# PSUM banks by role instead of by turn, in the groups of seven products

## The chip, the cores and the metric

The kernel runs on one core of a Trainium2 chip. The metric is the device time of one execution in microseconds (us), the median of several executions. A profile is one further execution that the hardware profiler recorded; its rows are in us from the start of the recorded span unless marked ns. Engine names are those of the profile: PE is the matrix engine's matmuls, PEld its weight loads (they run beside the matmuls), ACT the scalar engine, DVE the vector engine, POOL the GpSimd engine, SP the engine that issues most DMAs.

## The reference

One normalised input `xn = layernorm(x)` of 2048 tokens and 576 features goes through two branches, whose results are added to `x`.

```python
def _A_ref(x, wqkv, wo):      # 32 heads of 18; each token sees 8 tokens, 2 apart
    ...
    return o @ wo
def _B_ref(x, w1, w2, w3, w4):
    h = _gelu(_layernorm(x) @ w1)
    ...                       # four quarters of h shifted by +1, -1, +2, -2 tokens
    x1 = x + hs @ w2
    h2 = _gelu(_layernorm(x1) @ w3) @ w4     # 576 -> 4608 -> 576
    return x1 + h2
return x + _A_ref(xn, A_wqkv, A_wo) + _B_ref(xn, B_w1, B_w2, B_w3, B_w4)
```

The change lies in the last matmul pair, `gelu(layernorm(x1) @ w3) @ w4`, which is the largest part of the work.

## The kernel before

**Stages.** The order of the instructions on each engine is written out by hand. In time there come: the qkv projection, the mixing with `w1` and `w2`, the large MLP with the attention running on DVE beside it, and at the end the projection with `wo` (L1298 to L1325) with the output. All matmuls take their operands as a high and a low part, each in a reduced float format.

**The MLP in two forms.** The 36 blocks of 128 hidden features are taken as 18 pairs. The first 12 pairs (`NPL`) are computed directly. The last 6 pairs (`NWP`) are computed in groups, one per pair and half of the tokens: 12 groups, `q` = 0 to 11, in the loop at L1110. A group is a fast 2x2 scheme (after Strassen and Winograd) that needs seven block products in place of eight. Each product (`product`, L1051) is seven matmuls of 128x512 into one PSUM bank. Sums of weights and of inputs were made ahead (`combine`, `sums`), so a group is seven products with some additions of their results.

**Results and banks.** The seven products go to three banks:

- `ca` takes P1, then P6, P7 and P4 are added onto it, one after the other. Between them ACT copies out what stands there: `keep(Z1, ca)` after P1, `keep(Z2, ca)` after P6, `keep(Z3, ca)` after P7. Each later product onto `ca` therefore waits for the copy before it. What stands there after P4 is one quarter of the result: at the head of the next group ACT applies gelu to it twice (`gelu_ps("c21", ca, Z4)`, L1115, the instructions of L783 and L784), and that is the last use of the bank.
- `cb` takes P2 alone; DVE adds it to Z1 (`z_add(Z1, cb, Z1)`).
- `cc` takes P5, is read by DVE (`z_add(Z3, cc, Z3)`), has P3 added onto it, and is read by DVE for the last time in `z_add(Z2, cc, Z2)`.

A counter hands out four banks in turn (`cc0` to `cc3`, L1054 and L1055). With three requests per group, the bank that `cb` of a group gets is the one that `ca` of the group before had; `cc` gets the one that `cb` of the group before had, and `ca` gets the one that `cc` had two groups before. A first matmul into a bank waits until the bank's last reader is done.

**Order within a group.** Between the products stand up to eight `down` steps (L807), D0 to D7, which multiply the hidden features of the group before by `w4`: twelve matmuls of 128x288 each into one of two double banks, read out by DVE (L827) or by ACT into a staging tile (L823) that a POOL DMA adds onto `yd` in HBM (L824). The order is a string:

```python
ORDER = "P1 P2 P6 P5 P7 D0 P4 D1 P3 D2 D3 D4 D5 D6 D7"
ORDERS = {0: "P1 P2 D0 P6 P5 P7 D1 D2 P3 P4 D3",
          1: "P1 P2 D0 P6 D1 P5 P7 D2 P4 D3 P3 D4 D5 D6 D7",
          NWP - 1: "P1 P2 P6 P5 P7 D0 P4 P3 D1 D2 D3 D4 D5 D6 D7",
          NWP: "D0 D1 P1 P2 D2 P6 D3 P5 P7 D4 P4 P3 D5 D6 D7"}
```

Other work is hung on these steps by a plan (L1153 to L1237): the gelus of the finished quarters (`gelu_z`, L789 and L790, with `low_part`, L794, on DVE), the loads and the splitting of weights (`split_w4`, L562 and L564; `split_a` and `split_s`, L911 to L916), and in groups 2, 3, 5 and 6 `split_op` (L876 to L880), which splits the inputs of the second half of the tokens. ACT and DVE execute all this strictly in the order in which it is issued.

After group 11 come the last `gelu_ps` (L1267), eight last `down` steps (L1277) and the projection with `wo`.

Of the kernel before, what the change touches and what calls it, by code (L numbers as in the profile page):

```python
# [8 lines left out]
F32 = mybir.dt.float32  # L9
# [48 lines left out]
def fused_block(ctx, tc, x, wqkv, wo, w1, w2, w3, w4, out):  # L58
# [376 lines left out]
    T4 = mpool.tile([128, S + 4], F32R, name="T4")  # L435
# [180 lines left out]
    for t in range(NT):  # L616
        ps = psb.tile([128, 2, 512], F32, name="ps", tag="b")
# [169 lines left out]
    def gelu_z(name, z):  # L787
        h = hp.tile([128, 2, 512], F32R, name=name, bufs=2 if name == "c11" else 1)
        act.activation(h[:, 0, :], z, AF.Gelu_apprx_tanh)  # L789
        act.activation(z, z, AF.Gelu_apprx_tanh)  # L790
        return h

    def low_part(h, g):
        dve.tensor_tensor(h[:, 1, :], g, h[:, 0, :].bitcast(F32), op=ALU.subtract)  # L794
# [7 lines left out]
        h = hid[u, i] = gelu_ps((("c12", "c22"), ("c21", "c11"))[u % 2][i], ps, g)  # L802
        low_part(h, g)

    nps = [0, 0]

    def down(t, parts, pd):  # L807
        col = slice(t % 4 * 128, (t % 4 + 1) * 128)
        if pd is None:
            nps[0] += 1  # L810
            ps = qpd.tile([128, 2, 512], F32, name=f"ps{nps[0] % 2}")
        else:
            ps = pd.tile([128, 2, 512], F32, name="ps", tag="b")
        seq = []
        for h, w in parts:
            seq += [(h[:, 0], w, 0), (h[:, 0], w, 1), (h[:, 1], w, 0)]
        for n, (h, w, p) in enumerate(seq):
            for k in range(2):
                pe.matmul(ps[:, k, :HF], h[:, col], w[:, p, k * HF:(k + 1) * HF],  # L819
                          start=n == 0, stop=n == len(seq) - 1)  # L820
        if t in YD:
            e = staging()
            act.copy(e.rearrange("p (h c) -> p h c", h=2), ps[:, :, :HF])  # L823
            pool.dma_start(yd[t], e, accum_op=ALU.add)  # L824
        else:
            yv = Y[:, t, :].rearrange("p (h c) -> p h c", h=2)
            dve.tensor_tensor(yv, ps[:, :, :HF], yv, op=ALU.add)  # L827
# [215 lines left out]
    qpc = qpcc.__enter__()  # L1043
# [4 lines left out]
    SLOT = {"A11": 0, "A22": 1, "A12": 2, "S1": 0, "S3": 1, "S2": 2, "S4": 3}  # L1048
    WX = {}

    def product(w, xk, onto=None, last=False):  # L1051
        ps = onto
        if ps is None:
            nps[1] += 1  # L1054
            ps = qpc.tile([128, 512], F32, name=f"cc{nps[1] % 4}")  # L1055
        for i, (a, v) in enumerate(HALVES):
            k = 128 if a else 96
            pe.matmul(ps, WX[w][:k, v, SLOT[w], :], area[sb][xk][:k, a, :],  # L1058
                      start=onto is None and i == 0, stop=last and i == len(HALVES) - 1,
                      skip_group_check=True)  # L1060
        return ps

    def keep(z, ps):
        act.copy(by_token(z), in_order(ps))

    def z_add(dst, ps, z):
        dve.tensor_tensor(by_token(dst), in_order(ps), by_token(z), op=ALU.add)
# [42 lines left out]
    for q in range(NQ):  # L1110
# [126 lines left out]
            at("P5", lambda: read_xo(1, ring_block(("o", 1))))  # L1237
        for it in ORDERS.get(q, ORDER).split():
            if it == "P1":
                ca = product("A11", "B11")  # L1240
                keep(Z1, ca)
                if q:
                    low_part(h21, Z4)
            elif it == "P2":
                cb = product("A12", "B21", None, True)
                z_add(Z1, cb, Z1)
            elif it == "P6":
                product("S2", "T2", ca)
                keep(Z2, ca)
            elif it == "P5":  # L1250
                cc = product("S1", "T1")
                h11 = hid[q, "c11"] = gelu_z("c11", Z1)
            elif it == "P7":
                product("S3", "T3", ca)
                keep(Z3, ca)
                z_add(Z3, cc, Z3)
                low_part(h11, Z1)
            elif it == "P4":
                product("A22", "T4", ca, True)
            elif it == "P3":  # L1260
                product("S4", "B22", cc, True)
                z_add(Z2, cc, Z2)
            else:
                down(*prev[int(it[1])], None)
            for f in plan.get(it, ()):
                f()
# [31 lines left out]
    for t in range(NT):  # L1298
# [14 lines left out]
        if t < NT - 1:  # L1313
            ps = psb.tile([128, 2, 512], F32, name="ps", tag="b")
# [40 lines left out]
```

## Time and profile before

| | us |
|---|---|
| median of 3 runs | 1297.74 |
| lowest and highest of them | 1296.04, 1299.88 |
| the profiled execution's own time | 1297.46 |
| its recorded span | 1295.7 |
| PE busy | 1274.2 |
| DVE busy | 921.3 |
| ACT busy | 558.4 |
| POOL busy | 214.4 |

The twelve groups take the stretch from 925.67 us to 1218.34 us of the span. In a row of the timeline stand the start, the length, the engine, the line, the operation, the tiles written and read, the shape and the count of merged instructions; in brackets at the end stands the time that the engine sat idle before it and what ended that. A row of waits gives the total, the count and the longest. Matmuls are pipelined, so the lengths of consecutive ones overlap and the distance of their starts is what counts.

### The profile page before, as it was taken

The page shows a single profiled execution, that of the slowest core. Times are in us where ns is not written, and L with a number is a line of the kernel's source. Part 1 is how long each engine was busy: PE and PEld are TensorE (multiplying, and loading weights), DVE is VectorE, ACT ScalarE, POOL GpSimd, SP SyncE. Part 2 cuts the span into 40 slices and gives each one's busy share as a digit, 9 for nine tenths or more (in the row PEclk, how much of TensorE's full clock was granted, in tenths as well). Part 3 has the DMA queues.
Part 4 walks back from the last instruction along what each step waited for, and adds up shares of the span by engine and source line. Part 5 has one row for each costly group of instructions (what it writes and reads, how often), then busy time and mean ns, then how long its engine had stood idle before and what let it go on. Part 6 is the DMA issues. An engine that isn't in the chain of part 4 may idle for free. (4 is left out here: it accounts for less than half of the span.)

```text
span 1295.7 us, 19586 instructions
## 1 busy us (share of the span) xinstructions
PE 1274.2 (98%) x7594; PEld 1168.2 (90%) x7594; DVE 921.3 (71%) x1307; ACT 558.4 (43%) x900; POOL 214.4 (17%) x318
## 2 busy tenths in 40 slices
PE   8999999999999999999999999999999999999998
PEld 8999998898898999999998989988888898898998
DVE  6456534778568999999999999976855656676441
ACT  4322226526634434343434343434855466455530
POOL 2011100021221212221212221111111112112100
PEclk9999999999999999999999999999999999999999
DMA  7646874246896887986867877558747587788982
GB/s 209 155 115 142 171 169 144 72 140 173 199 261 142 179 195 156 190 172 136 187 142 157 172 142 153 97 108 194 195 78 156 111 192 144 164 202 180 260 255 82
DMA packets 196172, 210.21 MB, mean 162 GB/s; under 512 B 77920, under 2 KB 134176, under 8 KB 195952
## 3 DMA queue, kind: packets, MB, share of 16 engines
q1 hardware_dynamic: 165536, 144.82, 38.9%
q0 software_dynamic: 30544, 64.16, 32.0%
q8 instruction: 59, 0.97, 0.3%
q14 instruction: 33, 0.27, 0.1%
HBM read 112.98 MB, written 107.28 MB: 170 GB/s over the span
## 5 line engine op out<-in xcount | busy, mean ns | idle before, releaser
L819 PEld LDWEIGHTS ps<-w,c 128*128 128x128 f32 x3456 | 466.6, 188 | 15.0 <-DVE Y L827 4.7
L819 PE MATMUL ps<-w,c 128*128 128x288 f32 x3456 | 473.1, 294 | 6.1 <-DVE Y L827 3.5
L824 POOL DMA_DIRECT2D yd<-Y x125 | 109.2, 876 | 451.8 <-ACT Y L823 413.6
L823 ACT COPY Y<-ps 128x576 f32<-128x576 f32 x125 | 79.9, 640 | 162.6 <-PE ps L819 80.9
L794 DVE TENSOR_TENSOR c<-Y,c 128x512 fp32r<-128x512 f32 x144 | 98.9, 687 | 58.7 <-ACT Y L784 50.0
L783 ACT ACTIVATE c<-p 128x512 fp32r<-128x512 f32 x96 | 57.6, 600 | 190.8 <-PE p L800 190.8
L212 PE MATMUL ps<-WQ,xt 128*128 128x432 f32 x672 | 134.8, 360 | 0.0
L212 PEld LDWEIGHTS ps<-WQ,xt 128*128 128x128 f32 x672 | 125.6, 188 | 5.7
L726 DVE TENSOR_TENSOR prod<-q,k 128x1152 f32<-128x1152 f32 x64 | 86.6, 1353 | 11.1 <-DMA k<-qkvd 10.4
L827 DVE TENSOR_TENSOR Y<-ps,Y 128x576 f32<-128x576 f32 x108 | 81.1, 751 | 17.0 <-PE ps L819 16.8
L729 DVE TENSOR_REDUCE L<-prod 128x64 f32<-128x1152 f32 x64 | 86.4, 1351 | 1.1
L824 POOL DMA_DIRECT2D yd<-ev x55 | 47.8, 888 | 223.5 <-ACT ev L823 222.6
L800 PE MATMUL p<-xt,w3a 128*128 128x512 f32 x336 | 79.0, 391 | 1.4 <-ACT Y L784 1.4
L800 PE MATMUL p<-xt,w3s 128*128 128x512 f32 x336 | 78.6, 390 | 0.0
L800 PE MATMUL p<-x1n,w3a 128*128 128x512 f32 x336 | 78.5, 390 | 0.0
L800 PE MATMUL p<-x1n,w3s 128*128 128x512 f32 x336 | 78.5, 390 | 0.0
L705 DVE TENSOR_TENSOR prod<-v,L 128x1152 f32<-128x1152 f32 x56 | 75.8, 1353 | 0.8
L709 DVE TENSOR_TENSOR o<-o,prod 128x1152 f32<-128x1152 f32 x56 | 75.8, 1353 | 0.6
L800 PEld LDWEIGHTS p<-xt,w3a 128*128 128x128 f32 x336 | 62.2, 188 | 14.9 <-ACT Y L784 2.2
L119 POOL TENSOR_TENSOR rs<-rs,mhalf 128x1 f32<-128x1 f32 x48 | 31.0, 645 | 260.5 <-DVE rs L118 148.0
L800 PEld LDWEIGHTS p<-xt,w3s 128*128 128x128 f32 x336 | 62.4, 188 | 12.6
L800 PEld LDWEIGHTS p<-x1n,w3a 128*128 128x128 f32 x336 | 62.4, 188 | 12.6
(196 smaller groups left out, 1759.6 us busy)
## 6 DMA issues: line engine op xcount, KB each, us to landing
yd<-Y POOLq DMA_DIRECT2D x127, 288.0 KB, 5.4
yd<-ev POOLq DMA_DIRECT2D x55, 288.0 KB, 5.2
Y<-in_B_w_dram SPq DMA_DIRECT2D x23, 576.0 KB, 6.9
w3st<-in_B_w_dram SPq DMA_DIRECT2D x44, 256.0 KB, 6.0
qkvd<-stg SPq DMA_DIRECT2D x24, 432.0 KB, 3.5
xd<-st SPq DMA_DIRECT2D x16, 320.0 KB, 6.0
xd<-big SPq DMA_DIRECT2D x16, 320.0 KB, 7.5
xin<-in_A_x_dram SPq DMA_DIRECT2D x16, 288.0 KB, 3.9
```

Of the source, the lines that this page charges most:

```text
L212: pe.matmul(ps[:, h, :n], xs(a), ws(b, h), start=i == 0, stop=i == len(PAIRS) - 1)
L705: dve.tensor_tensor(dst, vv, Lf[:, :, w:w + 1].to_broadcast([128, TPP * GH, HD]), op=ALU.mult)
L709: dve.tensor_tensor(o, o, dst, op=ALU.add)
L726: dve.tensor_tensor(prod.rearrange("p (j h) d -> p j (h d)", h=GH), q, k[:, r0:r0 + TPP, :], op=ALU.mult)
L729: dve.tensor_reduce(Lf[:, :, w], prod, axis=AX.X, op=ALU.add)
L783: act.activation(by_token(h[:, 0, :]), in_order(ps), AF.Gelu_apprx_tanh)
L794: dve.tensor_tensor(h[:, 1, :], g, h[:, 0, :].bitcast(F32), op=ALU.subtract)
L800: pe.matmul(ps, W3[f][:, w, :], x1n[b][:, a, :], start=n == 0, stop=n == len(PAIRS) - 1)
L819: pe.matmul(ps[:, k, :HF], h[:, col], w[:, p, k * HF:(k + 1) * HF], start=n == 0, stop=n == len(seq) - 1)
L823: act.copy(e.rearrange("p (h c) -> p h c", h=2), ps[:, :, :HF])
L824: pool.dma_start(yd[t], e, accum_op=ALU.add)
L827: dve.tensor_tensor(yv, ps[:, :, :HF], yv, op=ALU.add)
```

## The change

The counter of banks goes. `product` is told the bank: `ca` takes bank 0 in even groups and bank 3 in odd groups, `cb` always takes bank 1 and `cc` always bank 2. Nothing else is altered: the order of the instructions on every engine is the same, and PE alone has other waits.

```diff
-    nps = [0, 0]
+    nps = [0]
...
-    def product(w, xk, onto=None, last=False):
+    def product(w, xk, bank=None, onto=None, last=False):
         ps = onto
         if ps is None:
-            nps[1] += 1
-            ps = qpc.tile([128, 512], F32, name=f"cc{nps[1] % 4}")
+            ps = qpc.tile([128, 512], F32, name=f"cc{bank}")
...
             if it == "P1":
-                ca = product("A11", "B11")
+                ca = product("A11", "B11", q % 2 * 3)
...
             elif it == "P2":
-                cb = product("A12", "B21", None, True)
+                cb = product("A12", "B21", 1, last=True)
...
             elif it == "P6":
-                product("S2", "T2", ca)
+                product("S2", "T2", onto=ca)
...
             elif it == "P5":
-                cc = product("S1", "T1")
+                cc = product("S1", "T1", 2)
...
             elif it == "P7":
-                product("S3", "T3", ca)
+                product("S3", "T3", onto=ca)
...
             elif it == "P4":
-                product("A22", "T4", ca, True)
+                product("A22", "T4", onto=ca, last=True)
             elif it == "P3":
-                product("S4", "B22", cc, True)
+                product("S4", "B22", onto=cc, last=True)
```

In the program before, the first matmul of P2 of groups 1 to 11 carries a wait for ACT (in group 1 for an earlier matmul too). In the changed program no matmul of P1, P2 or P5 of these groups carries a wait for the readers of its bank, since earlier waits cover them. The first matmul of D0 of group 1, which waited for DVE, waits for ACT instead. The waits of P6, P7, P4 and P3 stay as they were.

## The prediction

> **What bounds the kernel now.** I read the page's busy shares first, then the waits in the stretch of the twelve groups (915 to 1215 us), then PE's timeline there, and last what ACT did while PE waited.
>
> ```profile
> span 1295.7 us, 19586 instructions
> ...
> PE 1274.2 (98%) x7594; PEld 1168.2 (90%) x7594; DVE 921.3 (71%) x1307; ACT 558.4 (43%) x900; POOL 214.4 (17%) x318
> ```
>
> PE is busy for 1274.2 of 1295.7 us. Only PE's idle time, 21.5 us in all, can be won by moving waits.
>
> ```profile
> PEld cc L1058 <- ACT Y L784: 10.8, 10, 2.9
> ...
> PE cc L1058 <- ACT Y L784: 6.3, 8, 2.5
> ...
> PE ps L819 <- ACT ev L823: 0.4, 1, 0.4
> ...
> PE ps L819 <- DVE Y L827: 0.2, 1, 0.2
> ```
>
> In that stretch PE waits for hardly anything but one thing: the second of the two gelus that read the `ca` of the group before (L784). It is the last reader of the bank that P2 gets. Ten times the weight loads stand still for it, eight times a gap shows on PE, up to 2.5 us. These are the waits that the change takes out.
>
> A gap understates a stall, because a matmul's recorded length hides the first part. So I go by the distances of starts:
>
> ```profile
> 943.45 3.74 PE L1058 MATMUL cc<-x1n,w3a 128*128 128x512 f32 x14
> 947.03 1.75 PE L819 MATMUL ps<-w,c 128*128 128x288 f32 x12
> ...
> 967.81 1.79 PE L1058 MATMUL cc<-x1n,w3a 128*128 128x512 f32 x7
> 969.82 1.87 PE L1058 MATMUL cc<-x1n,w3a 128*128 128x512 f32 x7 [0.23 <-ACT Y L784]
> 971.53 3.39 PE L1058 MATMUL cc<-xt,w3s 128*128 128x512 f32 x14
> 974.76 1.77 PE L1058 MATMUL cc<-x1n,w3s 128*128 128x512 f32 x7
> ...
> 992.29 1.79 PE L1058 MATMUL cc<-x1n,w3a 128*128 128x512 f32 x7
> 996.53 1.86 PE L1058 MATMUL cc<-x1n,w3a 128*128 128x512 f32 x7 [2.46 <-ACT Y L784]
> 998.23 3.39 PE L1058 MATMUL cc<-xt,w3s 128*128 128x512 f32 x14
> ...
> 1045.69 1.79 PE L1058 MATMUL cc<-x1n,w3a 128*128 128x512 f32 x7
> 1047.70 1.87 PE L1058 MATMUL cc<-x1n,w3a 128*128 128x512 f32 x7 [0.23 <-ACT Y L784]
> ```
> ```profile
> 1095.21 3.79 PE L1058 MATMUL cc<-x1n,w3a 128*128 128x512 f32 x14
> 1098.84 3.45 PE L1058 MATMUL cc<-xt,w3s 128*128 128x512 f32 x14
> 1102.13 1.80 PE L1058 MATMUL cc<-x1n,w3s 128*128 128x512 f32 x7
> ...
> 1119.72 1.79 PE L1058 MATMUL cc<-x1n,w3a 128*128 128x512 f32 x7
> 1121.74 1.91 PE L1058 MATMUL cc<-x1n,w3a 128*128 128x512 f32 x7 [0.23 <-ACT Y L784]
> 1123.49 3.45 PE L1058 MATMUL cc<-xt,w3s 128*128 128x512 f32 x14
> ```
>
> Each pair of starts brackets two products. Undisturbed, two products (P6 and P5 of group 2) take 974.76 - 971.53 = 3.23 us; in the later groups (P6 and P5 of group 7) 1102.13 - 1098.84 = 3.29 us. P1 and P2 together take more, and the excess is the whole cost of the stall, the slow restart included:
>
> - group 1: 947.03 - 943.45 - 3.23 = 0.35 us (no gap shows on PE)
> - group 2: 971.53 - 967.81 - 3.23 = 0.49 us
> - group 3: 998.23 - 992.29 - 3.23 = 2.71 us
> - group 5: the start of P2 after that of P1 is 2.01 us, as in group 2, so 0.49 us
> - group 7: 1098.84 - 1095.21 - 3.29 = 0.34 us
> - group 8: 1123.49 - 1119.72 - 3.29 = 0.48 us
>
> Groups 4 and 9 to 11 I take from the lengths of whole groups, cut from one P1 to the next:
>
> ```profile
> 992.29:1018.99 26.70, 24.24 (x148) 21.84 (x147) 15.48 (x26) 15.06 (x25) 4.32 (x5) 1.00 0.70 133
> 1018.99:1045.69 26.70, 24.24 (x148) 21.84 (x147) 16.00 (x26) 15.08 (x25) 4.53 (x6) 1.00 0.59 105
> ...
> 1119.72:1144.38 24.66, 24.43 (x148) 21.84 (x147) 16.80 (x32) 12.87 (x22) 4.34 (x6) 1.00 0.91 211
> ...
> 1193.68:1218.34 24.66, 24.43 (x148) 21.85 (x147) 10.78 (x16) 11.96 (x20) 4.47 (x6) 1.00 1.00 253
> ```
>
> The columns are length, then busy time of PE, PEld, DVE, ACT and POOL, then granted clock, DMA share and GB/s. Group 4 is as long as group 3, so 2.71 us again; groups 9 to 11 are as long as group 8, so 0.48 us each. Group 6 has no stall (two `down` steps stand ahead of its P1). All stalls together: 0.35 + 0.49 + 2.71 + 2.71 + 0.49 + 0.34 + 4 x 0.48 = **9.0 us**. That is the most that the change can give.
>
> **The change, part by part.** *Removed:* the wait at the head of P2 in eleven groups. The instructions and their order are otherwise the same on every engine, the DMAs included, so nothing has to be paid for in instructions.
>
> *What is late next.* P2 is followed by P6, which adds onto `ca` and waits for `keep(Z1, ca)` (L1064), the copy that ACT does straight after the two gelus. This is the step where a removed stall can come back. The worst case is group 3:
>
> ```profile
> 991.05 1.04 ACT L876 ACTIVATE xt<-xt 128x1024 fp32r<-128x1024 f32 x1
> ...
> 994.87 0.63 ACT L823 COPY ev<-ps 128x576 f32<-128x576 f32 x1
> ...
> 995.89 0.58 ACT L784 ACTIVATE Y<-cc 128x512 f32<-128x512 f32 x1
> 996.37 0.58 ACT L1064 COPY Y<-cc 128x512 f32<-128x512 f32 x1
> ```
>
> Here ACT works from 991.05 on without a gap: `split_op` of group 2 stands in front (its first row is shown), so the read-out of D7 at 994.87, the gelus and the copy all come late. The gelu ends at 996.47 and P2 starts at 996.53, so PE follows ACT by 0.06 us. The copy ends at 996.95, and none of this ACT work depends on P2. With the wait gone P2 would start 1.62 us after P1 (half of 3.23), at 993.91, and P6 would be ready at 995.52; but it can start only at 996.95 + 0.06 = 997.01. Before, it started at 998.23. The stall moves from P2 to P6, where it lasts 1.5 us, and 1.22 us are won. The restart is paid again: after the stall seven matmuls took 998.23 - 996.53 = 1.70 us in place of 1.62, so 0.08 us. **Net 1.14 us, not 2.71**, and the same in group 4.
>
> In group 8 the copy comes in time:
>
> ```profile
> 1121.56 0.61 ACT L1064 COPY Y<-cc 128x512 f32<-128x512 f32 x1
> ```
>
> It ends at 1122.17. P6 would start at 1123.49 - 0.48 = 1123.01, so 0.8 us are to spare and the whole 0.48 us is won. Group 2 and 5 are alike with the same rows on PE; group 1 has D0 between P2 and P6, and group 7's stall is shorter than group 8's.
>
> *Moved:* the waits of P5. Its bank is now the `cc` of the group before, last read after P3, not the `cb` read after P2. The nearest pair is P3 of group 6 and P5 of group 7:
>
> ```profile
> 1090.65 0.69 DVE L1067 TENSOR_TENSOR Y<-cc,Y 128x512 f32<-128x512 f32 x1 [1.04 <-PE cc L1058]
> ```
>
> DVE is done at 1091.34, and P5 follows P6 of 1098.84 by 1.65 us, at 1100.49: 9.1 us to spare, so cost 0. In group 1 the wait of D0 for ACT is for work of group 0, long done; also 0.
>
> The Trainium skill (Perfetto Trace Analysis, section "Matmuls") says that independent matmul groups should rotate through the PSUM banks, so that reading out one lies beside the matmuls of the next. That speaks against fixing `cb` and `cc` to one bank each; with the 9.1 us of the row above the sum by it stays the same here, since the read-out is over long before the bank comes round.
>
> *Beside it:* P2 now writes one bank while ACT reads another in the gelus. The gelu with PE waiting took 0.58 us (995.89); in group 8, where the first 0.3 us of it lie beside P1, the copy took 0.61 us. So ACT may lose 0.03 us an instruction, some 0.1 us of groups 3 and 4 each; within the range.
>
> *Where time that was won can be lost again.* ACT's chain in group 5 and the tail:
>
> ```profile
> 1057.46 1.06 ACT L876 ACTIVATE x1n<-x1n 128x1024 fp32r<-128x1024 f32 x1 [2.43 <-DMA x1n<-xn]
> ...
> 1060.85 0.64 ACT L823 COPY ev<-ps 128x576 f32<-128x576 f32 x1 [1.02 <-PE ps L819]
> ```
> ```profile
> 1223.50 0.64 ACT L823 COPY Y<-ps 128x576 f32<-128x576 f32 x1 [0.52 <-DMA yd<-Y]
> ```
> ```profile
> 1224.19 1.85 PE L819 MATMUL ps<-w,c 128*128 128x288 f32 x12 [0.93 <-ACT Y L823]
> ```
>
> In group 5 ACT waits for a DMA that P1 releases, so it doesn't come earlier with P2. But the next piece of ACT waits 1.02 us for PE, more than the 0.49 us won there: the chain starts with PE, and moves with it. In the tail PE loses 0.93 us to a read-out that waits for a DMA from the staging tile. That DMA follows D5 of group 11, which itself moves with PE, so the loss stays the same size. If either chain held on to the DMAs ahead of it, at most the 0.49 us of group 5 and the 0.48 us of group 11 would be lost.
>
> **Sum.** 0.35 + 0.49 + 1.14 + 1.14 + 0.49 + 0.34 + 4 x 0.48 = **5.9 us**. The profiled execution took 1297.46 us (span 1295.7), so 1291.6; its time is 0.3 us under the median of the three runs, 1297.74, which gives 1291.8. I say **1291.7**.
>
> **The rivals.**
>
> 1. *The stall moves whole to P6 in the short cases too.* Then only groups 3 and 4 give 1.14 us each: gain 2.3, time 1295.4. For it: the same ACT queue releases both. Against it: the 0.8 us to spare in group 8. It decides if ACT's copy ends 0.8 us later than in the rows.
> 2. *The chains of group 5 and of the tail hold.* Gain 5.9 - 0.97 = 4.9, time 1292.8. For it: the DMA share in both stretches is high (1.00 in group 11). Against it: the 1.02 us of ACT's wait for PE.
> 3. *Slower: the tail's DMAs.* D1 after group 11 needs the staging tile that D5 of group 11 filled. The chain of waits has that transfer:
>
> ```profile
> 1216.41 6.99 DMA yd<-Y
> ```
>
>    With PE earlier against the loads that SP issued, more of these transfers stand in the queues together. If this one took over 6.99 + 5.9 = 12.9 us, PE would lose more in front of D3 than it had won; at 17 us the time is 1301.6, 4 us slower. Against it: the loads of SP follow PE too, and only 0.48 us of the shift is not shared.
> 4. *The clock.* If the granted clock fell after the two new stalls at P6, the product behind each would take twice 1.62 us: gain 5.9 - 3.2 = 2.7, time 1295.0. In all rows above it is 1.00, and after the stall of 2.46 us the next product took 1.70 us, not 3.2. The Trainium skill (TensorE: Matmul & The Clock Gate, "A second HAM failure mode: psum-queue depth-cycling") tells of a kernel that cycles through PSUM banks, where short idle times between groups let the gate swing between half and full rate. By that rule the old stalls would have shown a throttled product behind them, and the trace doesn't agree.
> 5. *It doesn't do what it says:* another wait at the same place (an operand of P2) holds it. Then 1297.6. The operands of P2 are ready in the stall-free group 6, so it is unlikely.
>
> **How the numbers follow.** About 0.3%, 3.9 us, is what a measurement of this kernel can tell from no change. Forecast 0.72, rival 1 0.10, rival 2 0.08, rival 3 0.04, rival 4 0.03, rival 5 0.03. Faster by over 0.3%: forecast and rival 2, less a hundredth for a forecast that falls short, 0.79. Within: rivals 1, 4 and 5 and that hundredth, 0.17. Slower: rival 3, 0.04. The range goes from 9.0 us won, less what the runs scatter in the other direction, 1289.0, to 1295.5, which takes in rivals 1, 2 and 4.
>
> **What would show it.** Right: no wait of P2 for L784; a stall of about 1.5 us at P6 of groups 3 and 4 behind L1064, and none at P6 elsewhere; groups 8 to 11 of 24.2 us, groups 3 and 4 of 25.6; PE idle before D3 of the tail about 0.9. Wrong: waits of P6 in more groups (rival 1), the gap in the tail above 1.4 us (rivals 2 and 3), a granted clock under 1.00 (4).

## The result and the profile after

| | before | changed |
|---|---|---|
| median, us (6 runs each) | 1298.05 | 1289.88 |
| lowest and highest | 1296.04, 1299.88 | 1289.18, 1291.18 |
| the profiled execution | 1297.46 | 1290.47 |
| its span | 1295.7 | 1288.7 |

The ratio is 0.9939 with a 95% interval of 0.9926 to 0.9952: faster by 6 to 10 us. The forecast was 1291.7, 5.9 us less than before; the median fell by 8.2. The profile's mean clock of 0.999 comes from its end alone: the granted clock stands at 1.00 until 1287.3 us, and the last matmul ends at 1285.1.

The page of the changed kernel, with the line of busy times:

```profile
span 1288.7 us, 19585 instructions
...
PE 1272.9 (99%) x7594; PEld 1169.8 (91%) x7594; DVE 920.9 (71%) x1307; ACT 558.3 (43%) x900; POOL 214.2 (17%) x318
```

The same work in 7.0 us less. The waits of the changed kernel in the stretch of the groups (905 to 1208 us):

```profile
PEld cc L1057 <- ACT Y L1063: 3.5, 2, 1.7
...
PE cc L1057 <- ACT Y L1063: 2.6, 2, 1.3
...
PE ps L819 <- ACT ev L823: 0.4, 1, 0.4
```

All ten waits for L784 are gone. Two new ones stand there, for L1063 (`keep`, L1064 before): P6 of groups 3 and 4. PE's timeline for groups 2, 3 and 8:

```profile
966.86 3.40 PE L1057 MATMUL cc<-x1n,w3a 128*128 128x512 f32 x14
970.10 3.39 PE L1057 MATMUL cc<-xt,w3s 128*128 128x512 f32 x14
...
990.86 3.40 PE L1057 MATMUL cc<-x1n,w3a 128*128 128x512 f32 x14
995.57 3.50 PE L1057 MATMUL cc<-xt,w3s 128*128 128x512 f32 x14 [1.32 <-ACT Y L1063]
998.91 1.77 PE L1057 MATMUL cc<-x1n,w3s 128*128 128x512 f32 x7
```
```profile
1115.08 3.40 PE L1057 MATMUL cc<-x1n,w3a 128*128 128x512 f32 x14
1118.31 3.39 PE L1057 MATMUL cc<-xt,w3s 128*128 128x512 f32 x14
1121.54 1.77 PE L1057 MATMUL cc<-x1n,w3s 128*128 128x512 f32 x7
```

P1 and P2 are now merged into one row of 14 matmuls in every group. In group 3 the stall has moved behind them: P6 would have been ready 3.23 us after P1, at 994.09, and starts at 995.57, 1.48 us late. ACT in that place:

```profile
994.47 0.58 ACT L784 ACTIVATE Y<-cc 128x512 f32<-128x512 f32 x1
994.94 0.57 ACT L1063 COPY Y<-cc 128x512 f32<-128x512 f32 x1
```

The copy ends at 995.51 and P6 starts 0.06 us later. The lengths of the groups, cut at the starts of P1 as before (length, busy time of PE, PEld, DVE, ACT, POOL, granted clock, DMA share, GB/s):

```profile
990.86:1016.44 25.58, 24.26 (x147) 21.84 (x146) 15.39 (x26) 15.05 (x25) 4.32 (x5) 1.00 0.75 138
1016.44:1042.02 25.58, 24.26 (x147) 21.84 (x146) 15.92 (x26) 15.08 (x25) 4.52 (x6) 1.00 0.61 109
1115.08:1139.10 24.02, 24.02 (x148) 21.94 (x146) 16.80 (x32) 12.87 (x22) 4.33 (x6) 1.00 0.95 220
1187.14:1211.16 24.02, 24.02 (x148) 21.94 (x146) 10.77 (x16) 11.96 (x20) 4.46 (x6) 1.00 1.01 270
```

Groups 3 and 4 are 1.12 us shorter than before (26.70), groups 8 to 11 0.64 us shorter (24.66). The tail kept its wait, a little longer than the 0.93 us of before:

```profile
1217.19 1.85 PE L819 MATMUL ps<-w,c 128*128 128x288 f32 x12 [1.11 <-ACT Y L823]
```

Between profiles of the same kernel the lengths of most groups repeat to within 0.02 us, those of groups 3 and 5 to within 0.2, so they are the measure in what follows. Each is the distance from the start of a group's first matmul (P1, in group 6 D0) to that of the next group, in us, from the timeline of the one profile of each run:

| group | 1 | 2 | 3 | 4 | 5 | 6 | 7 | 8 | 9 | 10 | 11 |
|---|---|---|---|---|---|---|---|---|---|---|---|
| before | 24.35 | 24.48 | 26.70 | 26.70 | 25.40 | 24.12 | 24.51 | 24.65 | 24.65 | 24.65 | 24.65 |
| before, second profile | 24.35 | 24.48 | 26.85 | 26.73 | 25.40 | 24.12 | 24.51 | 24.65 | 24.65 | 24.65 | 24.65 |
| changed | 24.01 | 23.99 | 25.59 | 25.58 | 24.92 | 24.12 | 24.02 | 24.02 | 24.02 | 24.02 | 24.02 |
| cb on old ca | 24.38 | 24.49 | 28.30 | 26.72 | 25.39 | 24.11 | 24.38 | 24.63 | 24.63 | 24.63 | 24.51 |
| cb, cc swapped | 24.01 | 23.99 | 25.67 | 25.58 | 24.92 | 24.11 | 24.02 | 24.02 | 24.02 | 24.02 | 24.02 |
| stalls in 3, 4 | 24.01 | 23.99 | 28.29 | 28.15 | 24.92 | 24.13 | 24.02 | 24.02 | 24.02 | 24.02 | 24.02 |
| stalls elsewhere | 24.35 | 24.48 | 25.59 | 25.58 | 25.41 | 24.12 | 24.51 | 24.65 | 24.65 | 24.65 | 24.65 |
| copy first | 24.01 | 23.99 | 24.67 | 24.71 | 24.92 | 24.16 | 24.02 | 24.02 | 24.02 | 24.02 | 24.02 |
| and w4 later | 24.01 | 23.99 | 24.00 | 24.02 | 25.76 | 24.18 | 24.02 | 24.02 | 24.02 | 24.02 | 24.02 |

Before to changed these groups won 0.34 + 0.49 + 1.11 + 1.12 + 0.48 + 0.49 + 4 x 0.63 = 6.55 us. The rest of the 7.0 us between the two spans lies where the program is the same: the first product starts at 925.12 in place of 925.67 us, and the tail lost about 0.2. In the profiles of all runs that first start lies between 922.5 and 926.4 us, so it is scatter.

### The profile page after: what moved, and what is told of

It reads as the page before. It is cut to its first block, busy times and chain, and to the rows that moved or that the text cites. A ratio compares the mean times of both kernels' runs of the same rounds, so it can differ in the third digit from the quotient of the medians.

```text
span 1288.7 us, 19585 instructions
## 1 busy us (share of the span) xinstructions
PE 1272.9 (99%) x7594; PEld 1169.8 (91%) x7594; DVE 920.9 (71%) x1307; ACT 558.3 (43%) x900; POOL 214.2 (17%) x318
## 5 line engine op out<-in xcount | busy, mean ns | idle before, releaser
L819 PEld LDWEIGHTS ps<-w,c 128*128 128x128 f32 x3456 | 466.7, 188 | 14.3 <-DVE Y L827 4.2
```

## The experiments

**Theory:** the whole gain is the wait of P2 for the bank of the old `ca`, given back in part at P6 of groups 3 and 4. **Rivals:** the banks of `cb` and `cc`, or the pace of the matmuls, have a part in it; a long idle time of PE costs more than its length.

### The other profiles of the changed kernel, and of the kernel before

> The changed kernel once more, for a second profile. Theory (only the wait of P2 for the bank of the old ca was removed, and it comes back in part at P6 of groups 3 and 4): 1289.9 us, 0.994 of the kernel before; P1 and P2 without stall in all groups, stalls of 1.5 us at P6 of groups 3 and 4. Rival (part of the gain is the pace of the matmuls, which was 1.61 us a product in place of 1.65 in P6, P5 and P7 of groups 7 to 11, and the pace is chance of one execution): the second profile shows 1.65 us again in some groups.

Measured: 1289.02 us, ratio 0.9935 (0.9912 to 0.9958). P6 and P5 of groups 7 to 11 take 1.61 us each again; the slower pace of 1.65 us shows only behind P6's stall in group 3 (25.67 us), and in group 0.

> The changed kernel beside the three above on the same chip: 1289.9 us, 0.994 of the kernel before. Theory: no difference to its other runs beyond 0.3%. Rival: the pace of the matmuls in P6, P5 and P7 differs from profile to profile and moves the time by up to 0.5 us.

Measured: 1289.76 us, ratio 0.9937 (0.9924 to 0.9950). Same picture. The profiled execution took 1292.03 us, 1.5 us more than that of the run above; 1.3 us of these lie ahead of the first product, which starts at 926.43 us in place of 925.15.

> The changed kernel on the same chip. Theory: its stalls of 1.3 to 1.5 us at P6 of groups 3 and 4 never let the clock fall, so every execution has a mean clock of 0.999 or 1.000 (what is left under 1 lies after the last matmul); about 1289.5 us. Rival: some executions at 0.998 or less.

Measured: 1288.54 us, ratio 0.9925 (0.9911 to 0.9940), all six executions at a clock of 1.000. Of the 16 executions of the changed kernel in these three runs 15 had a mean clock of 1.000 and one 0.999. A mean of 0.999 can hide one fall of the clock (the profile of the next section has one) or none (the first profile of the changed kernel has none before its last matmul), so that one execution stays undecided.

> The kernel before itself, for a second profile and its executions' clocks. Theory: the profile shows the two stalls of 2.6 us and behind at least one of them, in most executions, matmuls at half the pace for one window of 3.4 us; ratio 1.000. Rival: clock 1.000 throughout and no half pace, as in its first profile, in all executions.

Measured: ratio 0.9996 (0.9984 to 1.0008). The second profile has a clock of 1.000 again, so it shows no half pace: the expectation for the profile missed. The list of executions has it: 7 of the 12 had a mean clock of 0.998 or 0.997, four had 1.000 and one 0.999. Over the three comparisons above, 28 of 44 executions of the kernel before had 0.998 or less, with a mean of 1298.6 us, and 9 had 1.000, with a mean of 1295.2 us; the other 7 had 0.999.

### One part undone: cb on the bank of the old ca

```diff
-                cb = product("A12", "B21", 1, last=True)
+                cb = product("A12", "B21", (q - 1) % 2 * 3, last=True)
```

> One part undone: cb takes the bank that ca of the group before had (0 or 3), ca and cc stay by role. Theory: the stall at P2 is back in the eleven groups, 2.6 us in groups 3 and 4 and 0.26 to 0.4 us in the others, plus the restarts; time as before, 1298 us (ratio 1.000 within 0.001). Rival (the fixed banks of cb and cc, or which bank a role has, set the pace of the matmuls): part of the gain stays, 1292 us or less.

Measured: 1297.48 us, ratio 1.0001 (0.9988 to 1.0013). The theory's number. Its waits and PE's timeline in groups 3 and 4:

```profile
PE cc L1057 <- ACT Y L784: 6.3, 8, 2.5
```
```profile
995.78 3.11 PE L1057 MATMUL cc<-x1n,w3a 128*128 128x512 f32 x7 [2.46 <-ACT Y L784]
998.69 3.79 PE L1057 MATMUL cc<-xt,w3s 128*128 128x512 f32 x14
1002.31 1.77 PE L1057 MATMUL cc<-x1n,w3s 128*128 128x512 f32 x7
...
1024.08 1.89 PE L1057 MATMUL cc<-x1n,w3a 128*128 128x512 f32 x7 [2.46 <-ACT Y L784]
1025.81 3.39 PE L1057 MATMUL cc<-xt,w3s 128*128 128x512 f32 x14
```

The stalls are the same to the digit (6.3 us, eight times). But look behind them. In group 4 P2 takes 1025.81 - 1024.08 = 1.73 us; in group 3, behind a stall of the same 2.46 us, it takes 998.69 - 995.78 = 2.91. That is 1.2 us more, and P6 is slower too: group 3 is 28.30 us long, 1.6 more than in the kernel before. This profile's mean clock is 0.999. The granted clock (third number from the end) is at half for 3.4 us in group 3, and at 1.00 all through group 4:

```profile
996.10:999.50 3.40, 3.40 (x9) 2.64 (x8) 0.86 (x2) 1.25 (x3) 0.00 (x0) 0.50 1.00 161
```

So the clock fell behind the one stall and not behind the other.

### The other part undone: cb and cc swap

```diff
-                cb = product("A12", "B21", 1, last=True)
+                cb = product("A12", "B21", 1 + q % 2, last=True)
...
-                cc = product("S1", "T1", 2)
+                cc = product("S1", "T1", 2 - q % 2)
```

> The other part undone: cb and cc swap banks 1 and 2 in alternate groups, ca stays by role. Theory: the banks of cb and cc have 9 us to spare either way, so nothing changes against the changed kernel: 1289.9 us, ratio to before 0.994. Rival (which bank a role has matters): off by over 1 us.

Measured: 1288.30 us, ratio 0.9939 (0.9916 to 0.9961), no group differs by over 0.1 us from the changed kernel. Fixing `cb` and `cc` is neither gain nor loss; what counts is that neither P1 nor P2 gets the bank of the old `ca`.

### The wait made longer: one bank for ca

```diff
-                ca = product("A11", "B11", q % 2 * 3)
+                ca = product("A11", "B11", 0)
```

> The same wait made longer: ca takes bank 0 in every group, so P1 itself waits for the gelus of the group before. Theory: P1 starts 0.06 us after the second gelu, which by the rows of the kernel before is 1.9 us late in groups 1 and 7, 2.0 in groups 2, 5 and 8 to 11, and 4.2 in groups 3 and 4, each with 0.1 us of restart; 25.4 us against no stall at all (1286.7), so 1312 us. Rival (a PE that idles that long comes back at a lower granted clock): the product after the stalls of 4.2 us takes 3.2 us in place of 1.7, and the time is 1315 us or more.

Measured: 1320.26 us, ratio 1.0183 (1.0149 to 1.0216), mean clock 0.991. The rival's number. PE's timeline in groups 3 and 4:

```profile
996.60 5.08 PE L1057 MATMUL cc<-x1n,w3a 128*128 128x512 f32 x14 [4.08 <-ACT Y L784]
1001.52 3.38 PE L1057 MATMUL cc<-xt,w3s 128*128 128x512 f32 x14
...
1026.52 5.76 PE L1057 MATMUL cc<-x1n,w3a 128*128 128x512 f32 x14 [4.08 <-ACT Y L784]
1032.12 3.39 PE L1057 MATMUL cc<-xt,w3s 128*128 128x512 f32 x14
```
```profile
1054.89 5.08 PE L1057 MATMUL cc<-x1n,w3a 128*128 128x512 f32 x14 [1.85 <-ACT Y L784]
...
1161.35 3.53 PE L1057 MATMUL cc<-x1n,w3a 128*128 128x512 f32 x14 [1.86 <-ACT Y L784]
```

P1 and P2 take 4.92 and 5.60 us behind the long stalls in place of 3.23, and the time is 8 us over the 1312 us that were reckoned for the stalls alone. The second fence shows the short stalls of groups 5 and 9, as long as each other: the row of the two products is 5.08 us long behind the one and 3.53 behind the other. The stalls of 1.85 us in groups 8, 10 and 11 look like that of group 5, the one of group 2 like that of group 9.

### Only the two long stalls, and only the short ones

```diff
-                cb = product("A12", "B21", 1, last=True)
+                cb = product("A12", "B21", (q - 1) % 2 * 3 if q in (3, 4) else 1, last=True)
```

> cb takes the bank of the old ca in groups 3 and 4 alone, bank 1 elsewhere: only the two long stalls of P2 (2.6 us) are back. Theory (each of these stalls costs 1.13 us of waiting over the changed kernel and, in most executions, also lets the granted clock fall to half for one window of 3.4 us, which is 1.6 us more): executions at a mean clock of 1.000 at 1291.8 us, others, at 0.999 to 0.997, up to 1295; the median 1293 to 1295. Rival (a long stall costs its length alone): all executions at a clock of 1.000 and 1291.8 us.

Measured: 1293.12 us, ratio 0.9965 (0.9950 to 0.9980); on the same chip the changed kernel took 1288.54, so the two stalls cost 4.6 us. All nine executions have a mean clock under 1.000, seven of them 0.998 or 0.997. Stretches of its profile, cut at the changes of the granted clock (the third number from the end), and PE's timeline in group 3:

```profile
995.60:999.00 3.40, 3.40 (x10) 2.62 (x9) 1.25 (x2) 0.86 (x2) 0.00 (x0) 0.50 1.04 170
999.00:1022.90 23.90, 21.73 (x135) 19.72 (x134) 13.42 (x23) 13.21 (x21) 3.79 (x5) 1.00 0.58 121
1022.90:1026.30 3.40, 3.12 (x7) 2.49 (x8) 0.81 (x2) 1.85 (x4) 0.54 (x1) 0.50 0.89 128
```
```profile
994.90 2.75 PE L1057 MATMUL cc<-x1n,w3a 128*128 128x512 f32 x7 [2.46 <-ACT Y L784]
997.45 4.13 PE L1057 MATMUL cc<-xt,w3s 128*128 128x512 f32 x14
1001.41 1.77 PE L1057 MATMUL cc<-x1n,w3s 128*128 128x512 f32 x7
```

Twice the clock stands at 0.50 for 3.4 us. In the first of these stretches lie 10 matmuls, where at 0.23 us each there would be 14 or 15. From the stall's end to P7 group 3 needs 1001.41 - 994.90 = 6.51 us, where the kernel before needed 1001.46 - 996.53 = 4.93 in its profile: 1.6 us for one fall of the clock. Of the two groups' 28.29 and 28.15 us, 26.70 is what a group with such a stall takes at full clock, as in the first profile of the kernel before; the rest, 1.6 and 1.45 us, is the clock.

```diff
-                cb = product("A12", "B21", 1, last=True)
+                cb = product("A12", "B21", 1 if q in (0, 3, 4) else (q - 1) % 2 * 3, last=True)
```

> The complement: cb takes the bank of the old ca in all groups but 3 and 4, so only the short stalls (0.26 to 0.4 us) are back. Theory: 0.34 us in group 1, 0.49 in groups 2 and 5, about 0.5 in groups 7 to 11, with 0.1 more where the pace of the next products is the slow one; 1289.5 + 3.8 to 4.3 = 1293.5 us, and no execution at a mean clock under 0.999. Rival (it is the many short stalls that let the clock fall): clocks of 0.998 and less here too, and a time above 1294.5.

Measured: 1292.99 us, ratio 0.9961 (0.9949 to 0.9974), 4.4 us over the changed kernel on that chip; seven of eight executions at 1.000 and one at 0.999. The groups' lengths are those of the kernel before except in 3 and 4, and the sum of their excess over the changed kernel is 0.34 + 0.49 + 0.49 + 0.49 + 4 x 0.63 = 4.3 us. Its waits:

```profile
PE cc L1057 <- ACT Y L1063: 2.6, 2, 1.3
PE cc L1057 <- ACT Y L784: 1.4, 6, 0.2
```

The short stalls cost what they last, with the slower pace behind them. The two halves add up: 4.6 + 4.4 = 9.0 us, where the kernel before lies 1297.91 - 1288.54 = 9.4 us over the changed one on this chip.

### What is left at P6: the copy first, and w4 later

```diff
-            h21 = gelu_ps("c21", ca, Z4)
+            old = ca
...
                 keep(Z1, ca)
                 if q:
+                    h21 = hid[g, "c21"] = gelu_ps("c21", old, Z4)
+                    prev += [(s0 + j, [(hid[g, "c11"], w0), (h21, w1)]) for j in range(4)]
                     low_part(h21, Z4)
```

> On top of the changed kernel ACT does the copy of Z1 after P1 ahead of the two gelus of the group before, not behind them. Theory (P6 of groups 3 and 4 waits for that copy, 1.5 us each): the copy comes 1.0 us earlier there, so P6 stalls 0.5 us in place of 1.5; 1288.0 us, 1.9 less than the changed kernel. Rival (the stall there is ended by something else that comes at the same time, or is given back later): no change, 1289.9.

Measured: 1286.65 us, ratio 0.9914 (0.9901 to 0.9928); the changed kernel beside it 1289.76. In the profile P6 of group 3 waits a fourth as long:

```profile
992.80 3.52 PE L1057 MATMUL cc<-xt,w3s 128*128 128x512 f32 x14 [0.35 <-ACT Y L1063]
```

Groups 3 and 4 are 24.67 and 24.71 us long, 0.92 and 0.87 less than in the changed kernel: 1.8 us, the theory's 1.9. The medians differ by 3.1 us, but the executions of the changed kernel beside it lie 4 us apart, so the profile is the better measure.

```diff
+            if q in (3, 4):
+                at("P1", split_w4, NPL + pair(q - 1), 0)
+                at("P2", split_w4, NPL + pair(q - 1), 1)
-            at("P1", load_w4, p)
+            at("P2" if q in (3, 4) else "P1", load_w4, p)
...
-            at("D6", split_w4, p, 0)
-            at("D7", split_w4, p, 1)
+            if q not in (2, 3):
+                at("D6", split_w4, p, 0)
+                at("D7", split_w4, p, 1)
```

> As the kernel with the copy first, and in groups 2 and 3 the splitting of w4 goes from D6 and D7 behind that copy into the next group (and the load of the next w4 behind it). Theory: the last 0.5 us of stall and its restart go in groups 3 and 4 as well; 1286.8 us, 3.1 less than the changed kernel, and PE shows no wait at P6. Rival: the split comes too late for D0, whose first matmuls then wait; 1288 us or more.

Measured: 1286.38 us, ratio 0.9909 (0.9894 to 0.9924). No wait is left at P6:

```profile
989.07 3.40 PE L1057 MATMUL cc<-x1n,w3a 128*128 128x512 f32 x14
992.30 3.38 PE L1057 MATMUL cc<-xt,w3s 128*128 128x512 f32 x14
```

Groups 3 and 4 are as short as the others (24.00 and 24.02), 1.4 us less than with the copy first alone. But group 5 is 25.76 us in this profile in place of 24.92, at D5 and D7, where PE waits for ACT's read-outs. In the next kernel's profile, which has the same program there, it is 24.93. ACT's first split in group 5, of this kernel and then of the next:

```profile
1050.33 1.06 ACT L876 ACTIVATE x1n<-x1n 128x1024 fp32r<-128x1024 f32 x1 [4.38 <-DMA x1n<-xn]
```
```profile
1049.63 1.06 ACT L876 ACTIVATE x1n<-x1n 128x1024 fp32r<-128x1024 f32 x1 [2.83 <-DMA x1n<-xn]
```

Here the load came later, and ACT had no pause left before its next piece: the mechanism of rival 2 of the prediction, in the profiled execution of this kernel, where it takes back 0.8 of the 1.4 us. Whether it did so in the other three is not known; the medians of this kernel and the one before are alike, 1286.38 and 1286.65 us.

```diff
-            EV[0] = (9, 11, 10, 15, 13)
+            EV[0] = (10, 15, 13, 9, 11)
```

> As the one before, and the staging tiles of the last eight down steps are taken in another order, so that D1 gets a tile without a transfer under way (15) in place of the one that D5 of group 11 filled (11). Theory: the 1.1 us that PE waits ahead of D3 and the 0.2 us ahead of the next step go; 1285.5 us. Rival: the DMAs of the tail are the bound there and PE waits for the next tile as long; 1286.8.

Measured: 1285.59 us, ratio 0.9903 (0.9890 to 0.9917), the fastest of all. Its waits from 905 to 1240 us:

```profile
PE ps L819 <- DVE Y L827: 0.4, 2, 0.2
PE ps L819 <- ACT ev L823: 0.4, 1, 0.4
PE ps L819 <- ACT Y L823: 0.3, 1, 0.3
```

Beside the profile of the kernel with w4 later, PE's wait in the tail falls from 0.9 to 0.3 us, and the stretch from the last group to the projection shrinks from 14.3 to 13.7 us; the medians differ by 0.8. So 0.6 to 0.8 of the 1.3 us that were expected came: the wait of 0.2 us for DVE stays, and the rest waits for ACT's splitting work in front of the read-out, not for a tile.

## Why the prediction came out as it did

- **What bounds the kernel.** Right: PE, and the wait for L784 alone. With it back (cb on old ca) all of the gain goes; with the other edit back nothing goes.
- **Groups 1, 2 and 5.** Forecast 0.35, 0.49 and 0.49; measured 0.34, 0.49 and 0.48.
- **Groups 3 and 4, the step from a stall at P2 to one at P6.** Forecast: 1.5 us of stall at P6 and 1.14 us won; measured 1.48 us, and 1.11 and 1.12 won. The copy behind the gelus is the next thing that is late, as the rows of ACT said.
- **Groups 7 to 11.** The mis-sized term of the sum: 0.34 + 4 x 0.48 = 2.26 us forecast, 0.49 + 4 x 0.63 = 3.01 measured. I took the undisturbed pace of two products, 3.29 us, from P6 and P5 of group 7, which stand behind a stall themselves. Undisturbed they take 1121.54 - 1118.31 = 3.23 us in the changed kernel. A stall there costs 0.06 us more at its place and slows P6, P5 and P7 by 0.03 us each. Both profiles of the kernel before and that of the short stalls show it in each of these groups, the changed kernel in none of them.
- **The moved waits of P5.** Right that they cost nothing; the swap of `cb` and `cc` shows the same from the other side.
- **ACT beside PE.** The 0.03 us an instruction did not show: the gelu and the copy of group 3 took 0.58 and 0.57 us. The reading behind it was wrong, too: the copy of group 8 (1121.56 to 1122.17 us) reads the result of P1, so it lies behind P1 and beside P2, which starts at 1121.74.
- **The chain of group 5 and the tail.** Right: group 5 won its whole 0.48 us, and the tail's wait stayed near its size, 0.93 to 1.11 us (0.9 to 1.4 in the other runs that leave the tail and P1's bank alone). Rivals 2 and 3 did not come about.
- **Rival 4, the clock.** Here a step failed. I wrote that the old stalls would have shown a throttled product behind them, and that the trace doesn't agree. The trace was of one execution, of the minority at full clock. In 28 of 44 executions of the kernel before the mean clock was 0.998 or less. The two long stalls alone brought that about in 7 of 9 executions and the short ones in none of 8, so it is the stalls of groups 3 and 4 that let the clock fall, for about 1.5 us each. The change takes that away: behind its stalls of 1.3 us at P6 no profile shows a fall, and 15 of 16 executions had 1.000. So the mechanism was at work, in the kernel before and not in the changed one, and it adds to the gain. Between executions at a clock of 1.000 the difference is 1295.2 - 1289.1 = 6.1 us, close to the sum of the groups; the rest of the measured difference is the clock.
- **The bound of 9.0 us.** It counted every stall at its length and so left the clock out as well. On the chip of the fourth run the changed kernel was 9.4 us faster, although its stalls at P6 bring some 3 us back.

So the forecast of faster was right and for its reasons; 5.9 us was too small by 0.7 us for the pace in groups 7 to 11 and by some 2 us for a cost of the long stalls that the first profile didn't show. That the range took this in is partly luck: its lower end, 1289.0, stands for the 9.0 us of all stalls with nothing given back at P6, and no term of it is the clock.

## What to carry to other kernels

A bank that goes on being added to has the latest last reader; give it banks of its own in alternate rounds, and banks with early readers need no turn. When a wait is taken away, read on the releasing engine when the next thing that the waiting engine needs is done: here the copy behind the gelus told to 0.03 us how much of 2.7 us would be won. Take the undisturbed pace from a place that no stall precedes, and look at the clocks of all executions, not of the profiled one alone, before a throttled clock is ruled out: the same stall can fall on either side of a window's edge.

## What the runs showed of the hardware

- An idle time of PE of 2.46 us (2.86 us from the last start to the next) halved the granted clock afterwards in some places and not in others. In the run with one bank for `ca`, 4.08 us did it both times, and 1.85 us in groups 5, 8, 10 and 11 but not in 2 and 9. Behind the 1.32 us of the changed kernel no profile shows it. A fall lasts 3.4 us; behind the 4.08 us of group 4 it lasted 6.8.
- The changes of the clock lie on a grid of time: in every profile they are whole multiples of 3.41 us apart (in the profile with the two long stalls the falls start 1022.90 - 995.60 = 27.3 us apart, eight times 3.41). Laid over the stalls, the grid tells where the clock falls. The fourteen profiles have 41 idle times of PE of over 0.9 us between 905 and 1240 us. In nine of them at least 1.85 us lie in one window of the grid, and the clock fell at the end of that window each time; in the other 32 at most 1.79 us do, and it never fell. With cb on the old ca the 2.46 us of group 3 lie in one window, those of group 4 are split into 1.79 and 0.67; in the first profile of the kernel before the two stalls are split into 0.75 and 1.71 and into 1.35 and 1.11. This is read from the traces; no run shifted a stall against the grid on purpose.
- The Trainium skill (TensorE: Matmul & The Clock Gate, section "What's actually happening") says that the gate follows a free-running window of about 3.4 us; the 3.4 us and the 27.3 us of this case agree. The rule that the Trainium skill has in that page's section "HAM oscillation — how this bites in real kernels", no PE idle gap over about 3.4 us, is too wide here: 2.46 us and even 1.85 us were enough, and the measurement decides.
- Behind a short stall the matmuls of the next three products went at 1.65 us a product in place of 1.61 in groups 7 to 11, but not in groups 2 and 5, in both profiles of the kernel before and in that of the short stalls; with cb on the old ca only in groups 8 to 10. The `down` step after them ended it. What sets the pace stays open.
